# Batch 1 of a strided sparse attention: the first pair's k cast one group earlier, the exponentials of its scores in one block

## The chip, the cores and the metric

One core of a Trainium2 chip runs the whole program. The metric is the device time of one execution in microseconds (us). TensorE is called PE here, its weight loads PEld, VectorE DVE, ScalarE ACT, GpSimd POOL, SyncE SP.

## The reference

Attention over q, k and v of shape (8, 8, 576, 64), followed by a two-layer network on the 4608 tokens.

```python
scores = (1.0 / np.sqrt(D)) * np.matmul(q, k.transpose(0, 1, 3, 2))
rel = pos[:, None] - pos[None, :]
mask_local = (rel >= 0) & (rel < 32)                                   # heads 0 to 3
mask_strided = (rel >= 0) & (pos[None, :] % 32 == pos[:, None] % 32)   # heads 4 to 7
attn = softmax(np.where(mask, scores, -1e9))
x = np.matmul(attn, v)      # as (4608, 512): token by head and column
h = x @ w_in                # 512 to 2048
g = np.maximum(h, 0.0) ** 2
out = g @ w_out             # 2048 to 512, float32
```

The real softmax subtracts the row's maximum and divides by the sum plus 1e-9.

## The kernel before

The kernel computes in bf16 with sums in float32 in PSUM. Its long part is the network: the 4608 tokens are nine chunks of 512. For each chunk `mm1` (L706) makes sixteen tiles of 128 hidden columns by 512 tokens, four matmuls each; ACT takes the ReLU out of PSUM (L712, called relu below) and DVE squares it (L713, called square below). `mm2` (L728) multiplies by w_out, four output tiles for each chunk, each in four parts of four matmuls. One `mm1` tile or one `mm2` part is a **group**. Groups are counted from 0 through the whole program: groups 0 to 15 are the hidden tiles of chunk 0 (the first five are made ahead), groups 16 to 31 its second layer, groups 32 to 47 the hidden tiles of chunk 1, and so on. Parts 0 to 3 of the second layer of chunk 0 are groups 16 to 19, 20 to 23, 24 to 27 and 28 to 31, and each reads another quarter of w_out.

The attention of the later batches is laid between the groups by a hand-written table, `PLAN`. A line "15: S4" says that step S4 is issued just before group 15. Every engine works its instructions in the order in which they are issued. Some work is put off: `later(n, ...)` issues it at the n-th tick from then, and a tick comes after each group.

The head pairs ("units") are numbered through: units 4 and 5 are the local heads 0 and 1, and 2 and 3, of batch 1. The steps that matter here are:

- `c4kv`: cast of unit 4's k (`cast_qk_local`, L296). The letter at the end is the engine, v for DVE, a for ACT. It reads a staging place in an xt tile that a DMA of POOL's fills, and writes k_l; despite the name the copy is bf16 to bf16. `c4qv`, `c5qv` and `c5ka` are its like.
- `T4kv`: six transposes on PE (L452) into a PSUM bank, and the copy out of it (L459) into kTl, the transposed k.
- `W1q0v` and the like: eight transposes (L320) of the strided heads' rows (q_t, k_t) of batch 1, and the copy out (L324) into qT_s or kT_s.
- `S4`: the scores of unit 4, twelve matmuls (L504) into four PSUM banks; then four exponentials on ACT (L520), one for each bank, and two multiplications with the mask on DVE (L526). `S5!` is the same for unit 5 in the other mode of the step.
- `D4.0`: attention times v for one head (L666), reciprocal and product on DVE (L671, L672).
- `k10v`, `k11v`: copies of the strided k into the block tile kb (L364, L367). `s1.0`: strided scores of batch 1 (L573), their exponential (L574) and mask (L576).
- `B10v`, `B11v`: two copies (L396) that spread the strided v (v_st, two DMAs at L389 and L392) into the block tile vb, for even and odd positions. `x1.0`: sums (L584) and products with vb (L587) of the strided scores, in group 24; the results pass through L589, L590 and L597.

PSUM has eight banks. The attention steps take theirs in turn from a small ring (`bank("pt")`); `mm1` takes two others in turn (`"ph"`), and so do two of the four output tiles of chunk 0. A bank that comes up again is written only when its last reader is done, so PE waits for that reader.

The two modes of the scores' step are these lines of `step_S`:

```python
        if mode == 1:
            for row in range(2):
                for half in range(2):
                    expo(row, half)
                later(row + 1, lambda row=row: masks(row), u)
            return
        expo(0, 0)
        later(1, lambda: expo(0, 1), u)
        later(2, lambda: (masks(0), expo(1, 0)), u)
        later(3, lambda: expo(1, 1), u)
        later(4, lambda: masks(1), u)
```

Of the kernel before, what the change touches and what calls it, by code (L numbers as in the profile page):

```python
# [27 lines left out]
5: o1 U1 mbg  # L28
6: o2 l2k8+9 mv0g o3 mk0g
10: c4qv  # L30
12: c4kv l2q8+9 T4qa
13: c5qv c5ka T4kv
14: W1q0v T5qa
15: S4
16: W1q1v T5ka
17: W1k0a W1k1v
18: S5! k10v
# [943 lines left out]
```

## Time and profile before

| what | us |
|---|---|
| median of three runs | 300.8 (300.67 to 301.02) |
| profiled execution: its own time | 299.94 |
| its span | 298.2 |
| PE busy | 289.5 (97%) |
| DVE busy | 178.2 (60%) |
| ACT busy | 172.5 (58%) |
| POOL busy | 72.3 (24%) |

The span is the time from the first to the last instruction in the trace; the execution's own time is a little longer. All times below are from the start of the span. The groups that the change touches run between 27 and 45 us. In the timeline a row gives start, duration, engine, line, operation and shapes, and in brackets how long the engine stood idle before it and what ended that. In the chain a row gives start, duration, engine and line of what held up the end of the run at that moment; "issue" is time for which the profile shows no reason. The granted clock of PE is 1.0 throughout.

### The profile page before, as it was taken

What the parts mean: (1) busy time and instruction counts of PE and PEld (TensorE: products, weight loads), DVE (VectorE), ACT (ScalarE), POOL (GpSimd) and SP (SyncE); (2) the same over time, 40 slices, a digit from 0 to 9 for tenths busy, and PEclk for the clock granted to TensorE, in tenths of its full rate; (3) what the DMA queues carried; (4) which work ended last, traced back from release to release, by engine and by line L of the source; (5) the groups of instructions that cost most, each with busy time, mean ns of one, the idle gap of its engine ahead of it and who ended that gap; (6) DMA issues with size and microseconds to landing.
All of it is one profiled execution on the core that took longest, in us unless ns stands there. A gap on an engine that the chain in (4) does not pass through costs nothing.

```text
span 298.2 us, 5651 instructions
## 1 busy us (share of the span) xinstructions
PE 289.5 (97%) x2136; PEld 146.4 (49%) x2172; DVE 178.2 (60%) x460; ACT 172.5 (58%) x325; POOL 72.3 (24%) x105
## 2 busy tenths in 40 slices
PE   7999999999999999999999999999999999999996
PEld 3654555545544544444455445544454444444444
DVE  5856689768768694598267955685484534104400
ACT  3858756686667735773477447645665257126511
POOL 8836634005504018073301730000000000000000
PEclk9999999999999999999999999999999999999999
DMA  7999999998999999999999999621011110010012
GB/s 155 176 209 203 193 199 188 164 202 148 128 146 191 164 200 166 151 154 134 191 135 164 130 206 164 101 57 70 35 23 54 66 42 0 35 73 36 0 70 73
DMA packets 93131, 37.28 MB, mean 125 GB/s; under 512 B 78956, under 2 KB 87238, under 8 KB 93104
## 3 DMA queue, kind: packets, MB, share of 16 engines
q0 software_dynamic: 54448, 18.82, 59.2%
q1 hardware_dynamic: 38512, 18.03, 32.6%
q8 instruction: 17, 0.28, 0.4%
q14 instruction: 10, 0.08, 0.1%
q10 hardware_dynamic: 144, 0.07, 0.1%
HBM read 38.21 MB, written 9.44 MB: 160 GB/s over the span
## 4 chain that ended last, share of the span: by engine, by line
PE 91%; ACT 3%; DVE 3%; issue 2%; DVEq 0%; ACTq 0%
PE psb L706 40%; PE psb L728 39%; PE psb L666 2%; PE psb L763 1%; PE psb L587 1%; PE psb L452 1%; PE psb L753 1%; PE psb L584 1%; PE psb L573 1%; ACT r L712 1%; PE psb L504 1%; ACT e L508 1%; PE psb L549 1%; DVE g_sb L713 1%; DVE xt L634 0%
## 5 line engine op out<-in xcount | busy, mean ns | idle before, releaser
L706 PE MATMUL psb<-xt,w_in_b 128*128 128x512 bf16 x558 | 132.1, 379 | 1.4 <-ACT xt L691 0.4
L728 PE MATMUL psb<-w_out_b,g_sb 128*128 128x512 bf16 x542 | 125.1, 379 | 1.3 <-issue 0.6
L712 ACT ACTIVATE r<-psb 128x512 bf16<-128x512 f32 x144 | 85.4, 599 | 38.2 <-PE psb L706 35.0
L713 DVE TENSOR_TENSOR g_sb<-r 128x512 bf16<-128x512 bf16 x144 | 60.8, 424 | 73.4 <-ACT r L712 72.6
L706 PEld LDWEIGHTS <-w_in_b 128*128 128x128 bf16 x576 | 53.4, 98 | 59.0 <-issue 1.6
L728 PEld LDWEIGHTS <-g_sb 128*128 128x128 bf16 x560 | 51.8, 98 | 57.2 <-DVE g_sb L713 0.3
L732 ACT COPY y<-psb 128x512 f32<-128x512 f32 x35 | 20.6, 590 | 53.2 <-PE psb L728 50.2
L597 DVE TENSOR_TENSOR xt<-psb,rv 64x144 bf16<-64x144 f32 x84 | 34.0, 405 | 8.0 <-ACT rv L590 6.9
L589 ACT ACTIVATE rv<-psb 128x432 f32<-128x432 f32 (+1 forms) x21 | 10.5, 501 | 9.8 <-PE psb L584 9.8
L672 DVE TENSOR_TENSOR x_l<-psb,rinv 96x384 bf16<-96x384 f32 x28 | 15.5, 554 | 1.0
L348 POOL DMA_DIRECT2D q_t<-in_q_dram x6 | 3.2, 540 | 43.5 <-DMA qT_s<-q_t 42.0
L603 DVE TENSOR_TENSOR xt<-psb,rv 64x270 bf16<-64x270 f32 (+1 forms) x28 | 10.9, 430 | 3.8 <-ACT rv L590 3.6
L574 ACT ACTIVATE e<-psb 128x432 bf16<-128x432 f32 (+1 forms) x21 | 10.4, 496 | 3.7 <-PE psb L573 3.7
L417 POOL DMA_DIRECT2D vl<-in_v_dram x7 | 10.3, 1474 | 9.0 <-DMA vl<-in_v_dram 7.2
L277 POOL DMA_DIRECT2D k_l<-in_k_dram x16 | 11.7, 737 | 2.4 <-ACT kTl L459 2.1
L277 POOL DMA_DIRECT2D q_l<-in_q_dram x16 | 11.7, 737 | 1.7 <-DMA k_l<-in_k_dram 1.7
L560 ACT ACTIVATE e<-psb 128x384 bf16<-128x384 f32 x24 | 9.6, 509 | 3.4 <-PE psb L549 3.4
L590 ACT ACTIVATE rv<-rv 128x432 f32<-128x432 f32 (+1 forms) x21 | 11.2, 533 | 0.7
L556 DVE TENSOR_TENSOR e<-e,mask_all 128x576 bf16<-128x576 bf16 x16 | 6.7, 458 | 6.9 <-ACT e L560 6.9
L666 PEld LDWEIGHTS <-e 128*128 128x128 bf16 x168 | 8.6, 101 | 4.6
L348 POOL DMA_DIRECT2D k_t<-in_k_dram x6 | 3.3, 557 | 28.2 <-DMA kT_s<-k_t 25.9
L666 PE MATMUL psb<-vl,e 128*128 128x65 bf16 x168 | 9.5, 195 | 0.1
(117 smaller groups left out, 217.5 us busy)
## 6 DMA issues: line engine op xcount, KB each, us to landing
out_dram<-y SPq DMA_DIRECT2D x35, 256.0 KB, 3.2
vl<-in_v_dram POOLq DMA_DIRECT2D x7, 384.0 KB, 13.2
w_out_b<-in_moe_w_out_dram POOLq DMA_DIRECT2D x4, 512.0 KB, 15.6
q_t<-in_q_dram POOLq DMA_DIRECT2D x7, 288.0 KB, 5.8
k_t<-in_k_dram POOLq DMA_DIRECT2D x7, 288.0 KB, 5.7
v_st<-in_v_dram POOLq DMA_DIRECT2D x7, 216.0 KB, 8.1
w_in_b<-in_moe_w_in_dram POOLq DMA_DIRECT2D x2, 704.0 KB, 13.5
k_l<-in_k_dram POOLq DMA_DIRECT2D x16, 72.0 KB, 8.1
```

The source lines that it names most:

```text
L277: nc.gpsimd.dma_start(out=t[:, :, hh, :], in_=src[b, 2 * p + hh].rearrange("(t p) d -> p t d", p=QL))
L589: nc.scalar.activation(rv, pn, AF.Ln)
L590: nc.scalar.activation(rv, rv, AF.Exp, scale=-1.0)
L597: nc.vector.tensor_tensor(to[:, :, NJ * part:NJ * (part + 1), par], of, by, op=ALU.mult)
L603: nc.vector.tensor_tensor(t, of[:, g:, :, lo:lo + k], by[:, g:, :, lo:lo + k], op=ALU.mult)
L666: nc.tensor.matmul(po[0:m, n, :], e[:, c:c + m], rhs[:, NL * part + n, 0:D + 1], start=True, stop=True)
L672: nc.vector.tensor_tensor(x, po[0:QL, :, 0:D], rinv[0:QL].to_broadcast([QL, NL, D]), op=ALU.mult)
L706: nc.tensor.matmul(ph, w_in_b[:, kk, 128 * ff:128 * (ff + 1)], xt[kk][:, 512 * c:512 * (c + 1)], start=(kk == order[0]), stop=(kk == order ...
L712: nc.scalar.activation(r, ph, AF.Relu)
L713: later(1, lambda: nc.vector.tensor_tensor(g[:, ff, :], r, r, op=ALU.mult))
L728: nc.tensor.matmul(py, g[:, ff, 128 * j:128 * (j + 1)], w_out_b[:, ff, :], start=(ff == 0), stop=(ff == 15))
L732: nc.scalar.copy(y, py)
```

## The change

Two entries of `PLAN` move; nothing else is edited.

```diff
 10: c4qv
-12: c4kv l2q8+9 T4qa
+11: c4kv
+12: l2q8+9 T4qa
 13: c5qv c5ka T4kv
 14: W1q0v T5qa
-15: S4
+15: S4!
 16: W1q1v T5ka
```

The cast of unit 4's k is issued before group 11 instead of before group 12. On DVE this puts it ahead of the square of group 11 instead of behind it. The other two steps of group 12, a load on POOL and the transposes of unit 4's q, stay where they are.

The "!" selects mode 1 for the scores of unit 4. On ACT the four exponentials now stand one behind the other ahead of relu 15; before, relu 15, the copy of `T5ka` and the copy of `W1k0a` stood between them. On DVE the first mask moves from behind the copy of `W1q1v` to ahead of square 15, and the second from behind `k10v` to ahead of the copy of `W1k1v`, behind that of `W1q1v`. The orders of PE, POOL and SP are the same in both kernels; only what some of PE's instructions wait for differs.

## The prediction

> **What bounds the kernel now.** I read the busy row first. PE is busy for 289.5 of 298.2 us, so an edit of VectorE (DVE) and ScalarE (ACT) can only help where it removes one of PE's few waits, and a removed wait only shortens the run if PE is not stopped again later by something that the edit does not move. The second reading was the chain that ended last, in order of time, through the stretch that the change touches.
>
> ```profile
> PE 289.5 (97%) x2136; PEld 146.4 (49%) x2172; DVE 178.2 (60%) x460; ACT 172.5 (58%) x325; POOL 72.3 (24%) x105
> ```
>
> ```profile
> 28.68 0.42 DVE g_sb L713
> 29.11 0.28 DVE k_l L296
> 29.38 0.05 issue
> 29.43 0.43 PE psb L452 x6
> ...
> 34.12 0.30 ACT e L520
> 34.43 0.53 ACT kTl L459
> 34.96 0.33 ACT e L520
> 35.28 0.04 issue
> 35.32 0.68 PE psb L320 x16
> ...
> 43.23 0.86 PE psb L728 x4
> 44.09 0.18 PE psb L584
> 44.28 0.21 PE psb L587 x8
> ```
>
> The chain leaves PE at two places that belong to the change. At 29.43 the transposes of the pair's k wait for its cast (k_l). At 35.32 the transposes of k_t wait for the third exponential, which must read a PSUM bank empty. From there to 44.49 it stays on PE. The third reading was the timeline without merging by chain, for what stands just beside PE at 44.
>
> ```profile
> 29.43 0.43 PE L452 MATMUL psb<-ident,k_l 96*128 96x96 bf16 x6 [0.29 <-DVE k_l L296]
> ...
> 35.32 0.68 PE L320 MATMUL psb<-ident,k_t 72*128 72x72 bf16 x16 [0.45 <-ACT e L520]
> ...
> 41.63 0.52 DVE L396 COPY vb<-v_st 54x1408 bf16<-54x1408 bf16 x1 [0.87 <-DMA v_st<-in_v_dram]
> ...
> 43.43 0.52 DVE L396 COPY vb<-v_st 54x1408 bf16<-54x1408 bf16 x1
> ...
> 44.01 0.37 PEld L587 LDWEIGHTS <-vb 128*128 128x128 bf16 x8 [0.19 <-DVE vb L396]
> ```
>
> The last three rows decide. The strided v of batch 1 (v_st) comes by DMA, VectorE spreads it into vb in two copies, and the weight load of L587 waits 0.19 us for the second one. In before that costs PE nothing, because the 182 ns of L584 hide it. It is a second path, paced by DMA, that reaches 44.1 at the same moment as PE's own path.
>
> **The k cast, a group sooner.** In before VectorE squares group 10 (27.82 to 28.24), then stands idle until relu 11 ends at 28.65, squares group 11 (28.68 to 29.11), and only then casts k_l (29.02 to 29.37, 349 ns). In after the cast goes into the idle 0.44 us. Its input is there: the trace's completion records have the load of k done at 27.49. So the cast runs from about 28.16 to 28.51, square 11 keeps its 28.68, and nobody on VectorE is later. PE's last matmul of group 12 starts at 28.76 and takes 0.215, so the transposes start at 28.97 instead of 29.43: PE gains 0.456 us.
>
> Part of that is lost at once. The next step on PE that needs a cast is the transposes of the second pair's q. With PE 0.456 earlier they would start at 30.82 - 0.456 = 30.36, but their cast (30.146 to 30.558) stands behind square 12, which waits for relu 12 (29.17 to 29.77); none of these moves. With the 57 ns that passed between the end of the k cast and its transposes, they start at 30.61. The lasting gain of this part is 30.82 - 30.61 = **0.21 us**. The cast and the squares make no DMA; POOL's and SP's orders do not change.
>
> **The four exponentials together.** In before ACT runs exponential 1, relu 15, exponential 2, the kTl copy, exponential 3 (34.83 to 35.27), the first kT_s copy, exponential 4 (36.32 to 36.73). In after the four stand together behind relu 14. Four such that follow each other in this trace (the second pair's, 37.136, 37.443, 37.734, 38.025) start 0.30 us apart. Relu 14 moves from 32.14 to 31.94 with the 0.21, so they start at 32.43, 32.73, 33.03 and 33.32. The third is done by 33.45, and PE can begin the k_t transposes straight after group 16, where its last matmul starts at 34.497 in before: 34.497 - 0.205 + 0.215 = 34.51 against 35.32. Of that 0.61 us are the wait, the rest the 0.21 from above. Input and bank are no obstacle: k_t landed at 33.18, and the first w_out piece, which group 16 reads, at 31.57.
>
> The bill is relu 15, which now stands behind three more exponentials: it starts at 33.32 + 0.29 = 33.61 instead of 33.53. Queued behind it is the kTl copy (34.10 instead of 34.31), so no loss. Who waits for relu 15 is group 17, which takes its PSUM bank: relu 15 ends at 34.21, group 17 begins at 35.03, cover 0.8 us; were the exponentials the 0.42 us apart that each lasts, relu 15 would end 0.36 later, still covered. Square 15 slips by 0.08 and is not read before group 28. The masks cost 450 ns each before and after. Mask 0 at 33.17 waits for exponential 2 and has only square 15 behind it. Mask 1 follows the W1q1 copy, ahead of the kT_s copy that waits for PE until 35.3 anyway. The scores of the second pair then start at 35.99 instead of 36.80, with all four banks read. **Sum: PE is 0.21 + 0.61 = 0.82 us early** from 36 us on.
>
> **Where it goes.** The 0.82 lasts only until PE meets something that has not moved. The first loads behind it are safe: v of batch 1 landed at 35.68 (wanted at 37.2), w_out's second quarter at 38.24 (wanted by group 20 at 39.48 - 0.82 = 38.66). Then comes x1.0 in group 24. Its second v_st transfer landed at 41.54, and the first vb copy began at 41.63. Behind it VectorE has no idle time: mask L576 to 42.44, reciprocal and product of the second pair (L671, L672) to 43.13, mask L576 to 43.42, second vb copy to 43.95. All inputs of these are there sooner in after, but the order is the same and the front of it waits for the DMA, so vb is again ready at 43.95, L587's weights load at 44.01 and its matmuls start at 44.11, as before. PE's L584 comes at about 43.2 (its bank is held by L672 until 43.13) instead of 43.93, and the time saved is spent waiting there. A second limit stands behind it: w_out's third quarter, for the L728 of group 24, landed at 44.06, and that matmul starts at 44.33. Even without the vb wait the gain there would be at most 0.25 us.
>
> The DMA path itself does not hurry with PE. From 25 to 50 us its mean busy share is over 1.2, and the POOL queue has eight transfers open, each next issue following a landing: q_t is issued at 36.23 after v's landing at 35.68, k_t at 38.80 after w_out's at 38.24. Beyond 44.33 VectorE runs about 0.5 us ahead (L597 starts when L672 is done, near 45.0, instead of 45.47), but PE meets hardly any wait between 44.3 and 63.2 that this could shorten. So the term for the end of the run lies between 0 (bound by vb) and -0.82 (no bound); I take 0 to -0.1, by the rows at 41.63 and 44.01. The profiled execution took 299.94 us for its span of 298.2; the runs shown have a median of 300.8, 0.86 above it, and I take the difference over unchanged.
>
> **Rivals.** *First, all of the 0.82 arrives.* This needs the second v_st transfer to land by 40.7 and w_out's third quarter by 43.5, 0.6 to 0.8 us sooner than in this trace. For it: the profiled execution is a single one, the runs spread by 0.35 us, and at 44.1 both paths tie, so any earlier landing goes to the gain. Against it: the transfers wait in a backlog of some 15 us (v_st's second was issued at 26.31), which the change does not touch. Time: 300.8 - 0.82 = 300.0.
>
> *Second, slower: the DMA path is pushed back.* The k cast moves from 29.02, where POOL was issuing w_out's third quarter (28.91 to 29.69), to 28.16, on POOL's L847 and L849 (27.83 to 28.65). The matching L847 and L849 at 27.20 and 27.55, which ran under another cast of this shape, took 0.28 and 0.23 us, so I see no lengthening. If it did hold POOL for its whole 0.35 us, w_out's third quarter would be issued at 29.26, and in the worst case land at 44.41; the L728 of group 24 would start about 44.46 against 44.33. That is +0.13; it decides from a slip of 0.22 us on. With the same slip at the other quarters, 301.2; for more than 0.6 us the backlog itself would have to drift by 0.8 us.
>
> The Trainium skill has a rule for this (page "SBUF — State Buffer", section "SBUF: two separate sides"): a VectorE copy in a two-port mode keeps GpSimd from writing descriptors while it runs. It would speak against this move, or for it, depending on which issue the cast falls upon; by the rows just given the cast leaves a descriptor-writing instruction and lands on affine selects, and these show no lengthening under a cast.
>
> *Third, the order does not do what it says*, because a wait on another engine keeps the exponentials apart. Each needs only its bank's scores and the cast only its load, so I see none; the time would be 300.8 as well.
>
> **How the numbers follow.** A measurement of this kernel can tell some 0.2% (0.6 us) from no change. Bound by vb or partly so, including the third rival: 0.77, with 300.7 as the likeliest time and 300.2 to 301.1 as its own range. All or most of 0.82 arriving: 0.17, at 300.0. Slower by over 0.6 us through the DMA path: 0.06. The range for 8 in 10 is 300.0 to 301.2, from the full gain to the slipping loads.
>
> **What would show it.** In the changed profile the wait before k_l's transposes (0.29) and before k_t's (0.45) is gone, a short new one stands before the second q's transposes near 30.6, scores of the second pair start near 36.0, and PE idles about 0.7 us ahead of L587, put down to vb or to the v_st transfer. I am wrong if L587 starts before 43.7, which means that v_st landed sooner or VectorE's row behind it is shorter, or if PE is not early at 36 at all.

## The result and the profile after

The changed kernel took 300.0 us in the median of 22 runs, the kernel before beside it 300.76; the ratio is 0.9975 with a 95% interval of 0.9966 to 0.9984. That is 0.75 us less (0.5 to 1.0): the first rival of the prediction, all of the 0.82 us arriving, and not its likeliest case (300.7). It is also the lower end of the prediction's range. The profiled execution took 298.88 us for a span of 297.2.

Lines of the changed kernel stand one further down than those of before (L453 for L452, and so on). The busy row hardly moves.

```profile
PE 289.2 (97%) x2136; PEld 146.0 (49%) x2172; DVE 177.9 (60%) x460; ACT 172.3 (58%) x325; POOL 72.4 (24%) x105
```

The chain that ended last, in order of time, in the changed kernel:

```profile
29.60 0.43 DVE g_sb L714
30.03 0.34 DVE q_l L297
30.41 0.43 PE psb L453 x6
...
34.42 0.52 PE psb L321 x16
...
42.16 0.86 PE psb L729 x4
43.03 0.18 PE psb L585
43.21 0.22 PE psb L588 x8
```

The chain no longer leaves PE for k's cast or for the third exponential. Up to 43 us it leaves PE once, from 27.83 to 30.41: over two relus with the copy of unit 4's qT between them on ACT, a square, and at the end the second pair's q cast, where the prediction had the new wait. The timeline, row by row:

```profile
27.96 0.40 DVE L297 COPY k_l<-xt 96x768 bf16<-96x768 bf16 x1
...
28.77 0.42 PE L453 MATMUL psb<-ident,k_l 96*128 96x96 bf16 x6
...
30.41 0.28 PEld L453 LDWEIGHTS <-q_l 96*128 96x128 bf16 x6 [0.21 <-DVE q_l L297]
...
32.23 1.31 ACT L521 ACTIVATE e<-psb 128x288 bf16<-128x288 f32 x4
...
34.25 0.69 PE L321 MATMUL psb<-ident,k_t 72*128 72x72 bf16 x16
...
35.74 0.43 PE L505 MATMUL psb<-qT,kTl 64*128 64x96 bf16 x12
...
40.48 0.56 DVE L397 COPY vb<-v_st 54x1408 bf16<-54x1408 bf16 x1 [0.78 <-DMA v_st<-in_v_dram]
...
42.33 0.52 DVE L397 COPY vb<-v_st 54x1408 bf16<-54x1408 bf16 x1
...
42.90 0.41 PEld L588 LDWEIGHTS <-vb 128*128 128x128 bf16 x8 [0.16 <-DVE vb L397]
43.05 0.38 PE L588 MATMUL psb<-e,vb 128*128 128x54 bf16 x8
```

The prediction had put L587 at 44.11, held by vb; here L588 stands at 43.05. The rows show what else moved: the first copy into vb begins at 40.48, not 41.63. The second v_st transfer landed at 40.39 us; in the profile of before it landed at 41.54. Again vb is ready at the very moment at which PE comes for it (0.16 us of a weight load's wait, hidden behind L585), but both are a microsecond sooner. So the first question was whether the landing had come forward by chance or through the change.

One execution differs from the next by up to 2 us before the changed stretch begins; what makes the difference is not followed up here. So I read PE's stretch from one fixed mark: the first transposes of unit 4's q (27.85 before, 27.65 after) to L587, L588 in the changed kernel. It is 44.11 - 27.85 = 16.26 us before and 43.05 - 27.65 = 15.40 us after, 0.86 shorter. From there to the end of the span it is 254.13 us in both profiles (298.24 - 44.11 and 297.18 - 43.05), so nothing behind L587 takes the gain away. In nine of the eleven further profiles it is 254.11 to 254.19 us as well; the two exceptions are named below.

### The profile page after: what moved, and what is told of

The parts are those of the page before. It is cut to its first block, busy times and chain, and to the rows that moved or that the text cites. A ratio compares the mean times of both kernels' runs of the same rounds, so it can differ in the third digit from the quotient of the medians.

```text
span 297.2 us, 5652 instructions
## 1 busy us (share of the span) xinstructions
PE 289.2 (97%) x2136; PEld 146.0 (49%) x2172; DVE 177.9 (60%) x460; ACT 172.3 (58%) x325; POOL 72.4 (24%) x105
## 3 DMA queue, kind: packets, MB, share of 16 engines
q0 software_dynamic: 54448, 18.82, 58.1%
## 4 chain that ended last, share of the span: by engine, by line
PE 92%; DVE 3%; ACT 2%; issue 2%; DVEq 0%; ACTq 0%
PE psb L729 39%; PE psb L707 39%; PE psb L667 2%; PE psb L453 1%; PE psb L764 1%; PE psb L588 1%; PE psb L505 1%; PE psb L754 1%; PE psb L585 1%; PE psb L574 1%; ACT r L713 1%; PE psb L550 1%; DVE g_sb L714 1%; PE psb L475 1%; PE psb L331 0%
## 6 DMA issues: line engine op xcount, KB each, us to landing
out_dram<-y SPq DMA_DIRECT2D x35, 256.0 KB, 2.8
```

## The experiments

Theory A: the transfers usually land early enough, the profile of before showed a late landing, and the gain is PE's own. Theory B: the landing is fixed by the program, and the change made the transfers faster. All measured ratios are against the kernel before on the same chip.

**The kernel before, again, and each half of the change alone.** The first run has no edit. The halves:

```diff
 # e2_cast_only, against before
-12: c4kv l2q8+9 T4qa
+11: c4kv
+12: l2q8+9 T4qa
 # e3_exps_only, against before
-15: S4
+15: S4!
```

> The kernel before, unchanged. Theory A (in a usual execution the DMA path to vb has room, and what one profile shows of its landing is chance): time within 0.1% of before; the landing of the second v_st transfer is not 41.54 us again but differs by some tenths or a whole us, and where it is later than 41.5, L587 waits and the span is longer by as much. Theory B (the DMA path is fixed by the program, and the change itself made it faster): time the same, the landing again at 41.5 us within 0.2, L587 at 44.1.

> Only the k cast a group sooner; the exponentials as before. PE early by 0.46 at k's transposes and by 0.21 from the second pair's q transposes on. Theory A: time -0.2 us (0.05 to 0.35). Theory B: 0 if v_st lands near 41.5, and -0.2 only with an earlier landing.

> Only the four exponentials together; the cast as before. The wait of k_t's transposes (0.61 us between matmul starts) goes. Theory A: time -0.6 us (0.35 to 0.75). Theory B: 0 to -0.1 if v_st lands near 41.5.

Measured: the kernel again 0.9994 (0.9977 to 1.0011), the cast alone 0.9994 (0.9973 to 1.0014), the exponentials alone 0.9986 (0.9961 to 1.0010). These intervals are wider than the effects; the times alone tell nothing apart here. The profiles do. In the unchanged kernel the transfer landed at 40.17, with the cast alone at 40.24, with the exponentials alone at 40.40. Theory B falls with the first of these: the same program put it 1.4 us sooner than its first profile. With the exponentials alone, vb and PE stand like this:

```profile
42.48 0.52 DVE L396 COPY vb<-v_st 54x1408 bf16<-54x1408 bf16 x1
...
43.93 0.35 PE L584 MATMUL psb<-e,ones_bd 128*128 128x432 bf16 x1
43.93 0.44 PEld L587 LDWEIGHTS <-vb 128*128 128x128 bf16 x8
44.11 0.38 PE L587 MATMUL psb<-e,vb 128*128 128x54 bf16 x8
```

vb is ready at 43.00, nearly 1 us before PE comes, and no weight load waits. From the mark to L587 it is 16.08 us with the cast alone (0.18 less than 16.26) and 15.65 with the exponentials alone (0.61 less). The terms of the prediction were 0.21 and 0.61.

The unchanged kernel, however, took 16.79 us on this stretch, 0.53 more than in its first profile. Its timeline shows why:

```profile
30.91 1.27 POOL L861 MEMSET vb<- 128x1408 f32 x1
...
31.19 1.20 DVE L296 COPY q_l<-xt 96x768 bf16<-96x768 bf16 x1
...
32.45 0.43 PE L452 MATMUL psb<-ident,q_l 96*128 96x96 bf16 x6 [0.41 <-DVE q_l L296]
```

The second pair's q cast, 0.41 us in the first profile, took 1.20 us. It began 0.28 us after a long memset of POOL's, and ended 0.21 us after the memset's end. In the first profile the cast began at 30.15 and the memset at 30.42: the cast was ahead.

**One cast more.** The wait that the change leaves, at the second q transposes, is taken away by moving that cast too.

```diff
 # e4_q_cast_too, against the changed kernel
-12: l2q8+9 T4qa
-13: c5qv c5ka T4kv
+12: l2q8+9 T4qa c5qv
+13: c5ka T4kv
```

> The changed kernel, and the second pair's q cast a group sooner as well, ahead of square 12 instead of behind it, so that the new wait of the second q transposes (0.2 us near 30.4) goes. Theory A: a further -0.2 us against the changed kernel, -0.95 us against before. Theory B: no gain over the changed kernel, -0.75 us.

Measured: 0.9959 (0.9936 to 0.9982), median 299.49 us. The cast took 0.35 us, no weight load waited for it, and the mark-to-L588 stretch was 15.28 us, 0.12 shorter than in the changed kernel. The direct gain is thus smaller than the 0.2 expected: the second q transposes came 0.25 us sooner from the mark (2.51 against 2.76), but those of k_t only 0.11 (6.49 against 6.60). In this one profile PE waited 1.10 us for a DMA of a later batch at 142.5, so it took 255.4 us from L588 to the end instead of 254.1.

**The vb wait made binding.** To see whether the wait on which the prediction rested is real, the two v_st loads go further back in POOL's queue, in both kernels alike.

```diff
 # e5_late_v_before against before, e6_late_v_after against the changed kernel
-5: o1 U1 mbg
-6: o2 l2k8+9 mv0g o3 mk0g
+5: o1 mbg
+6: o2 l2k8+9 U1 mv0g o3 mk0g
```

> The kernel before with the two v_st loads of batch 1 put behind w_out's third quarter and a load of batch 2 in POOL's queue, so that v_st lands some 4 us later and the copies into vb surely end behind PE's own path. Theory A (the wait for vb is real, it is only usually not the last to end): v_st's second part lands near 44, vb is ready 2.4 us behind that, L587 waits 1.5 to 2.5 us, time +1.5 to +2.5 us against before. Rival C (VectorE or PE work around it, so vb does not hold PE): less than +0.5 us.

> The changed kernel with the same later v_st loads. Theory A: PE is still 0.8 us early at 36 us, but all of it is spent waiting for vb: the same time as the kernel before with the later loads, within 0.2 us. Rival C: 0.75 us faster than that kernel.

Measured: 1.0128 (1.0098 to 1.0157) and 1.0163 (1.0136 to 1.0190), that is 3.8 and 4.9 us above before. With late loads the change brings nothing. That the changed kernel came out 1.1 us above the other and not within 0.2 was not expected; the two intervals overlap. The timeline of the kernel before with late loads:

```profile
47.13 0.34 PE L584 MATMUL psb<-e,ones_bd 128*128 128x432 bf16 x1 [1.80 <-DVE x_l L672]
47.97 0.39 PE L587 MATMUL psb<-e,vb 128*128 128x54 bf16 x8 [0.49 <-DVE vb L396]
...
47.96 0.28 PEld L587 LDWEIGHTS <-vb 128*128 128x128 bf16 x8 [2.91 <-DVE vb L396]
```

PE stops first at L584, whose bank is held by the product L672 behind the first vb copy, then at L587 for the second copy. The transfer landed at 45.48 and L587 started 2.49 us later; in the changed kernel with late loads it was 44.05 and 2.48 us; in the first profile of before 2.57. So where this path binds, L587 starts 2.5 us behind the landing, whatever PE did before. The cost exceeded the expected 1.5 to 2.5 us. In the profile of the kernel before with late loads the stretch from the mark (29.15) to L587 took 18.82 us, 2.56 more than 16.26; the rest lies ahead of the mark and was not followed up. In the changed kernel a further reason is in its profile. The windows of 2 us give PE's busy time in the second place and the granted clock behind the five engines:

```profile
44.00:46.00 2.00, 0.35 (x2) 0.00 (x0) 1.81 (x6) 0.00 (x0) 0.82 (x1) 1.00 1.30 196
46.00:48.00 2.00, 1.52 (x13) 0.73 (x13) 1.92 (x6) 1.09 (x2) 1.20 (x3) 0.77 1.30 212
48.00:50.00 2.00, 2.00 (x6) 0.76 (x5) 1.85 (x5) 0.00 (x0) 2.00 (x2) 0.50 1.28 184
50.00:52.00 2.00, 2.00 (x17) 1.03 (x15) 0.40 (x1) 1.09 (x2) 0.10 (x1) 0.88 2.19 159
```

After 1.65 and 0.48 us without work PE got half the clock. If it was either full or half, the means of the windows put this at about 47.1 to 50.5 us. The eight matmuls of groups 24 and 25 took 3.29 us instead of 1.89; from L588 to the end it took 256.0 us instead of 254.1. The other kernel waited as long (1.80 and 0.49) at a clock of 1.00; that its median is 304.1 where its profiled execution took 303.8 leaves open how often it was throttled.

**POOL's memsets put off.** The two long memsets near 30 and 32 us prepare the next batch. They go behind the loads of group 22, once in the changed kernel and once with the q cast moved too.

```diff
 # e7_memsets_later_after against the changed kernel;
 # e8_memsets_later_q_cast the same against e4
-6: o2 l2k8+9 mv0g o3 mk0g
+6: o2 l2k8+9 o3
-22: B11v l3k12+13 s1.2 U2
+22: B11v l3k12+13 s1.2 U2 mv0g mk0g
```

> The changed kernel with POOL's two long memsets (of the next batch's vb and kb, near 30.2 and 32.4 us) put off to behind the v_st loads of group 22. Theory L (a VectorE copy between SBUF tiles that starts while such a memset runs takes 1.2 us instead of 0.35, as one q cast did in the repeated run of before, and some executions pay for it): no cast over 0.45 us in the profile, time -0.1 to -0.4 us against the changed kernel. Rival: the slow cast was a rarity or hidden, time the same within 0.1 us.

> The changed kernel with the second pair's q cast a group sooner and the memsets put off. Theory A: -0.1 to -0.2 us against the changed kernel for the cast; with theory L nothing more, since the cast then stands ahead of the memset anyway; -0.9 to -1.2 us against before.

Measured: 0.9985 (0.9965 to 1.0006) and 0.9986 (0.9973 to 1.0000), medians 299.62 and 299.69 against 300.28. With the memsets gone no q or k cast was long (the stretch from the mark took 15.42 us in e7). But neither shows a gain over the changed kernel, which did not run beside them: their ratios lie within the intervals of the changed kernel's own. The second was expected 0.9 to 1.2 us below before and came out 0.4 below (0 to 0.8). What the memsets cost on average is not shown. In e8 the first vb copy fell on POOL's next long instruction, the issue of a v load:

```profile
39.69 1.44 POOL L418 DMA_DIRECT2D vl<-in_v_dram  x1
40.02 1.43 DVE L397 COPY vb<-v_st 54x1408 bf16<-54x1408 bf16 x1
```

**The changed kernel and the moved q cast once more, side by side, and a third profile of before.**

> The changed kernel, unchanged. Theory A, in the form the runs so far give it (L587 starts at the later of two times: PE's own, 15.4 us after the transposes of the first q in this kernel and 16.26 in the one before, or 2.5 us after v_st's second part lands): v_st lands between 39.5 and 41 us, PE's own path is the later one or within 0.2 us of it, and the time is 0.6 to 0.9 us below before. Theory B (the change made the transfers faster): the landing at 40.4 within 0.2.

> The changed kernel with the second pair's q cast a group sooner, beside the changed kernel on the same chip. Theory A: 0.1 to 0.3 us faster than the changed kernel; no wait at the second q transposes. Rival: no difference beyond the spread.

> One more look at the kernel before: how far the landing of v_st's second part and PE's own path lie apart. Theory A: PE's path ends later by some tenths to two us. Theory B: both at the same moment, as in the first profile.

Measured: the changed kernel 0.9989 (0.9961 to 1.0017), median 300.33 against 300.6; with the q cast moved too 0.9972 (0.9945 to 1.0000), median 299.92. Both were expected lower, the changed kernel by 0.6 to 0.9 us against before and the other by a further 0.1 to 0.3; neither difference is clear of the spread. The transfer landed at 40.01 and 40.26, and in the kernel before at 40.39. There the rows at the end of the stretch are:

```profile
42.72 0.52 DVE L396 COPY vb<-v_st 54x1408 bf16<-54x1408 bf16 x1
...
44.05 0.44 PEld L587 LDWEIGHTS <-vb 128*128 128x128 bf16 x8
44.24 0.38 PE L587 MATMUL psb<-e,vb 128*128 128x54 bf16 x8
```

vb was ready at 43.24, no weight load waited for it, and L587 started at 44.24, 16.26 us behind its mark (27.98): PE's own path, and the same 16.26 as in the first profile. The profile of the changed kernel met the memset this time:

```profile
30.02 1.27 POOL L862 MEMSET vb<- 128x1408 f32 x1
...
30.30 1.20 DVE L297 COPY q_l<-xt 96x768 bf16<-96x768 bf16 x1
...
31.56 0.43 PE L453 MATMUL psb<-ident,q_l 96*128 96x96 bf16 x6 [0.88 <-DVE q_l L297]
```

The transposes waited 0.88 us for the cast, and the stretch from the mark took 16.19 us instead of 15.40. That is 0.07 us less than an execution of before that is not hit, and 0.60 less than one that is (16.79). How often either is hit is not known: it was one of three profiles of before and one of two of the changed kernel with its usual loads. The form of theory A that was put down before these runs had no term for the hit. With the q cast moved the stretch took 15.27 us, as in its first run (15.28); in both runs that cast stood ahead of the memset.

The second interval of the changed kernel holds "no change" as well as the first result. The first, from 22 runs, is the narrower one, and the two are compatible; the size of the gain is known to some 0.3 us, not better. The version with the q cast moved has lower medians (299.49 and 299.92), but its intervals overlap with those of the changed kernel, and only the second stands beside it on one chip.

## Why the prediction was right or wrong, point by point

**The terms on PE's path were right.** The cast alone was to gain 0.21 and gained 0.18; the exponentials 0.61 and 0.61; together 0.82 and 0.86. The new wait at the second q transposes came at 30.41 with 0.21 us on the weight load. Relu 15 started at 33.39, covered as worked out, and the second pair's scores at 35.74, which is 8.09 us after the mark; the prediction's 35.99 - 27.85 is 8.14.

**The step that failed is "Where it goes".** It took one landing, 41.54 us, for a fixed time, concluded that "vb is again ready at 43.95", and so put the term for the end of the run at 0 to -0.1 us. The runs gave -0.75 us, the two profiles -0.86 from the mark to L587. The prediction's own sign of being wrong, L587 before 43.7, came true at 43.05, and the 0.7 us of idling ahead of L587 that it expected did not show: a weight load waited 0.16 us. The mechanism it had in mind exists: with late loads L587 starts 2.5 us after the landing and the change gains nothing. Its place in time was wrong. In the ten other profiles with the loads in their usual place the transfer landed between 39.49 and 40.78, in the two further ones of the unchanged kernel at 40.17 and 40.39, and the mark lay at 27.65 to 29.76. The first profile combined nearly the earliest mark with the latest landing, and so the tie of both paths at 44.1 was a chance of that execution. In the third profile of before vb had 1.0 us to spare against PE, which is more than the 0.86 that the change takes away.

A sign of it stood in the first profile: the two v_st landings lay 2.09 us apart (39.45 and 41.54) for 81 KB, while w_out's quarters of 512 KB landed 2.5 us behind their predecessors. In the profile after it was 1.39 us. Why that one transfer was slow is open.

**The first rival** had the right time (300.0), and its condition, a landing 0.6 to 0.8 us sooner, is what the runs show as usual. Its second condition, w_out's third quarter by 43.5, holds as well: that load landed at 44.06 in the first profile and at 42.02 to 43.23 in the ten others. The argument against it, that the change does not touch the backlog, was true and beside the point: the backlog did not have to move, it had to be known from more than one execution. **The range** held the time, at its lower end, because it reached to this rival; the likeliest time, 300.7, was worked out from the step that failed.

**The slower rival** expected the k cast to hold up POOL. No run shows that: in the profile after, the select beside the moved cast took 0.24 us as before, and w_out's third quarter was issued at 28.71, 1.06 us behind the mark as before (28.91). Elsewhere copies do hold POOL up: with the exponentials alone, the issue of an xt load took 1.02 us around the second vb copy, instead of 0.72. And the reverse happens: POOL's long instructions held up VectorE's copies, by 0.6 to 0.9 us. The change does not cause it, since the unchanged kernel had it too, but the q cast that may be hit stands where the change put the only remaining wait of PE in this stretch, so that a hit there delays PE by nearly all of the gain.

**The third rival** fell: the four exponentials stand together (32.23, 1.31 us for all).

## What to carry to other kernels

Where a gain is to be lost at a second path that ends at the same moment, ask how far that moment moves from one execution to the next: a DMA landing and a chain on PE that start from different loads drift against each other by a microsecond and more, while in these profiles PE's own stretch from the mark repeated within 0.1 us for the same kernel, except where a cast met a memset (0.5 and 0.8 us). Measure such chains from a mark inside the program, not from the start of the span. And look at what POOL does when a short VectorE copy stands on the critical path.

## What the runs showed of the hardware

A VectorE copy between SBUF tiles that began 0.28 us after the start of a long POOL memset, or 0.42 after it, ended 0.21 us after the memset: it took 1.20 us instead of 0.35 (two profiles), and 1.06 in a third, of the changed kernel with late loads. Beside the issue of a v load (L417), usually 1.44 us long, it depended on where the copy into vb or kb began. In the thirteen traces together, six copies that began 0.32 to 0.67 us into the issue ended only after it: 1.17 us instead of 0.24 for one into kb (cast alone), 1.09 and 1.43 instead of 0.52 for two into vb (the q cast moved, without and with the memsets put off). Six that began 0.02 to 0.20 us into it kept their time, and the issue ended 1.05 us behind them; with the exponentials alone it took 1.73 us for that. Multiplications and copies out of PSUM that ran beside the same memsets kept their 0.42 and 0.74 us. The Trainium skill, page "SBUF — State Buffer", section "Who interferes with whom", says that copies and casts in a two-port mode and GpSimd exclude each other, that whichever starts first keeps the ports for its whole instruction, and that the other stands still. The rows of the memsets agree, and they show the side of the rule that the prediction did not apply. Those of the issues agree if an issue takes the ports some 0.2 to 0.3 us after its start and not at once; this is an estimate from these twelve copies.

Half the clock was granted after a wait of 1.65 and 0.48 us with 0.35 us of work between, about 2.5 us in all, and lasted some 3.4 us. The Trainium skill, page "TensorE: Matmul & The Clock Gate", section "What's actually happening", puts the fall of the clock after an idle window of about 3.4 us; here less was enough once, and a wait of the same length in the sister kernel was not.
